# Attention given out in slices of one tile, by running sums of two engines' work, with the norm multiplied on ScalarE

## The chip, the cores and the metric

One core of a Trainium2 chip runs the whole program. Its engines are TensorE (PE: matmuls; PEld is its weight load), VectorE (DVE), ScalarE (ACT), GpSimd (POOL) and SyncE (SP), which here issues nearly all DMAs. Each engine works through its own instructions in the order in which the program issues them to it. The metric is the device time of one execution in microseconds, lower is better.

## What is computed

```python
kv = np.einsum('bhsd,bhse->bhde', k, v)            # 8 batches, 8 heads, 576 rows, 64 features
out = np.einsum('bhsd,bhde->bhse', q, kv)
rms = np.sqrt(np.mean(out * out, axis=-1, keepdims=True) + 1e-06)
x = (out / rms * g_norm)                           # then (B,H,S,D) -> (B*S, H*D): 4608 x 512
h = x @ w_in                                       # 512 x 2048
g = np.maximum(h, 0.0) ** 2
return g @ w_out                                   # 2048 x 512
```

A linear attention, normed per head, feeds a feed-forward block of two matrix products with a squared relu between them. All is fp32; the weights arrive in fp64.

## The kernel before

**Tiles and strips.** The 4608 tokens are 36 tiles of 128 tokens; a batch has 4 full tiles and half of a fifth, which two batches share (the rest tile). Four tiles are a strip, so there are nine strips, 0 to 8. The feed-forward block runs strip by strip: a first half (`up`, x times w_in) and a second half (`down`, g times w_out). Strip 0 multiplies plainly going up; strip 1 goes up in 28 steps of one Strassen product each (`up`, seven products for each of four groups); strips 2 to 8 go up with Strassen twice over, in 55 slots (`up_slot`, `up_small`): seven sets of seven small products, set n starting in slot 7n and its products in every second slot. The second halves have 14 steps (`down`, `down_deep`). The w_in and w_out sums for this are made in strips 0 and 1 by VectorE and GpSimd and streamed back from DRAM in `w_blk` tiles.

**Banks.** Each product of strips 1 to 8 lands in one of three PSUM banks, A, B and C, of a pool of five (`fpsum`). A bank holds several products one after the other, so a product in bank A can only start when the one before it there has been read: by a ScalarE copy (`snap`, line 1153, or 743 in strip 1) or by a VectorE add (line 1148, or 796 in strip 1). In strip 1 the order of the products of a group is 1, 2, 6, 5, 7, 3, 4, of which 1, 6, 7 and 4 use bank A.

**Attention for the coming strips** is cut into slices, a list of functions with arguments that is built once (lines 638 to 689) and worked off by `attend` between the feed-forward's steps. For tiles from batch 2 on, the slices are:

- `transposed_query` (T): VectorE transposes a head pair's queries, line 383, and for the last pair of an odd batch also the rest tile's, line 387. The query is loaded by small DMAs that are let go one at a time (`drip`), at most one in a step, and only where no key load is due; a T whose loads have not yet been issued issues them itself. Each T puts the load of three pairs later on that list.
- `key_value` (K): k times v on PE (line 431), copied to SBUF by ScalarE (lines 436 and 437). Its successor's keys are loaded one or two steps after it.
- `query`: for a pair of tiles, an optional K, then q times kv on PE into two banks `x_ps` (line 467, one buffer), then ScalarE squares the two tiles into SBUF (line 476).
- `mean_roots`: VectorE sums the squares by head (line 484), scales (485), and ScalarE takes the root (490) into a PSUM tile.
- `normalized`: VectorE inverts the root and refines it with one Newton step on tiny operands (lines 495 to 499), then multiplies each of the pair's tiles by it out of PSUM (line 535).
- `squares_x`: VectorE transposes a tile in 32 x 32 blocks (line 602); `send_x` stores it to DRAM, and some steps later `fetch_x` loads it as the feature-major x of a strip.

The first batches go another way: `roots_normalized` does the norm in one slice, and `features` transposes the normed tile on PE (line 595).

**What sets their order.** All engines get their instructions in the order of this one program, so a slice stands on each engine's queue between what the step before it and the step after it issue. In strips 1 to 8 a fixed pace gives the slices out by count: after step i of a strip those up to

```python
pace = 25 if s == DEEP else 36
attend(begun + (goal - begun) * min(i + 1, pace) // pace)
```

where `begun` is the list's place at the strip's start and `goal` the place that the next strip needs (`ready`), or more in later strips. Strip 1 (`DEEP`) works off 24 slices in its first 25 steps, strips 2 to 7 between 13 and 23 each in their first 36 slots.

Of the kernel before, what the change touches and what calls it, by code (L numbers as in the profile page):

```python
# [10 lines left out]
FP32 = mybir.dt.float32  # L11
# [3 lines left out]
AF = mybir.ActivationFunctionType  # L15
ALU = mybir.AluOpType
AX = mybir.AxisListType
# [3 lines left out]
def kernel(  # L21
# [34 lines left out]
    nc = tc.nc  # L56
    P = 128
    B, H, S, D = q.shape
# [3 lines left out]
    NP = H // 2  # L62
# [10 lines left out]
    DEEP = 1  # L73
    DEEP_UP = 2
    SQ = 32
    Q_ON_PE = 2
    X_ON_PE = 2
    EPS = 1e-6
    const = ctx.enter_context(tc.tile_pool(name="const", bufs=1))
# [6 lines left out]
    small = ctx.enter_context(tc.tile_pool(name="small", bufs=3))  # L86
# [10 lines left out]
    apsum = opening.enter_context(tc.tile_pool(name="opsum", bufs=2, space=bass.MemoryType.PSUM))  # L97
# [381 lines left out]
    def mean_of(sqs):  # L479
        ms = small.tile([P, 2, H], FP32, name="ms", tag="ms")[:, : len(sqs)]  # L480
        for i, sq in enumerate(sqs):
            if len(sq.shape) == 3:
                sq = sq.rearrange("p r e -> p (r e)")
            nc.vector.reduce_sum(out=ms[:, i], in_=by_head(sq), axis=AX.X)
        nc.vector.tensor_scalar(out=ms, in0=ms, scalar1=1.0 / D, scalar2=EPS, op0=ALU.mult, op1=ALU.add)
        return ms

    def root_of(ms, ps=None):
        r = ps if ps is not None else small.tile([P, 2, H], FP32, name="rms", tag="rms")[:, : ms.shape[1]]
        nc.scalar.activation(r, ms, AF.Sqrt)  # L490
        return r
# [10 lines left out]
    queried = []  # L502
# [12 lines left out]

    def roots_normalized(ns):
        parts, ms = queried.pop()
        queried.append((parts, (ms, root_of(ms))))
        normalized(ns)

    def mean_roots(ns):
        parts, sqs = queried.pop()
        ms = mean_of(sqs)
        r = apsum.tile([P, 2, H], FP32, name="root", tag="at")[:, : len(ns)]
        queried.append((parts, (ms, root_of(ms, r))))

    def normalized(ns):
        parts, means = queried.pop()
        r = inverse_root(*means)
        for i, n in enumerate(ns):  # L530
            x_n[n] = xn_pool.tile([P, d_model], FP32, name="x_n", tag="x_n")
            o = x_n[n].rearrange("p (q r d) -> p r q d", r=2, d=D)
            x = parts[i].rearrange("p r (q d) -> p r q d", d=D)
            w = r[:, i].rearrange("p (r q) -> p r q", r=2).unsqueeze(3).to_broadcast([P, 2, NP, D])
            nc.vector.tensor_tensor(out=o, in0=x, in1=w, op=ALU.mult)

    first = {}
    TAG_UP = "ABAC"
# [125 lines left out]
    T, K, last = transposed_query, key_value, query_pairs(1)[2]  # L664
    slices += [(query_means, (last,)), (K, (2, 0, 1)), (T, (2, 0)), (roots_normalized, (last,)), (T, (2, 1))]
    slices += [(T, (2, 2)), (features, (last[0],)), (T, (2, 3)), (K, (2, 2, 3))]
    for b in range(2, B):
        pairs = query_pairs(b)
        for i, pair in enumerate(pairs):
            left = len(pairs) - i  # L670
            more = b + 1 < B
            at = left + (b == 2)
            keys = (b + 1, *{2: (0, 1), 1: (2, 3)}[at]) if more and at < 3 else ()
            if i == 0 and b > 2:
                slices += [(T, (b, p)) for p in (2, 3)]
            if i == 0 and b == 3:
                slices.append((K, (3, 2, 3)))
            slices.append((query, (pair, *keys)))
            if more and left == 1:
                slices.append((T, (b + 1, 1)))  # L680
            slices.append((mean_roots, (pair,)))
            slices.append((normalized, (pair,)))
            if more and left == 2:
                slices.append((T, (b + 1, 0)))
            slices += [(squares_x, (n,)) for n in pair]
            for n in pair:
                slices.append((send_x, (n,)))
                if n % NT == NT - 1:
                    ready[n // NT] = len(slices)
    slice_at = [0]  # L690

    def attend(n):
        while slice_at[0] < min(n, len(slices)):
            fn, a = slices[slice_at[0]]
            fn(*a)
            slice_at[0] += 1

    def out_rows(n):

# [486 lines left out]
    for s in range(N_STRIP):  # L1186
# [19 lines left out]
        goal, begun = ready.get(s + 1, len(slices)), slice_at[0]  # L1206
        if s >= DEEP_UP:
            goal = max(goal, min(ready[DEEP_UP] + (len(slices) - ready[DEEP_UP]) * (s - 1) // (N_STRIP - DEEP_UP - 1), len(slices)))
        total, done = sum(w for w, _, _ in steps), 0
        for i, (w, fn, a) in enumerate(steps):  # L1210
            if s == 0 and i < n_up:

                if 4 <= i < 10:
                    convert(3 + i)
                if i == 0:
                    load_next()
                    load_rest(1, nc.sync)
                    load_next()
                if i == 1:
                    load_next()  # L1220
                if i == 2:
                    for b in range(2):
                        load_q_rest(b, nc.sync)
                if i == 14:
                    for b in range(2):
                        store_first(b)
            elif s == 0 and i == n_up:
                convert(len(conversions))
                conv.close()

                stream_pool = ctx.enter_context(tc.tile_pool(name="stream", bufs=4, reuse_waits="tile"))
                sum_pool = ctx.enter_context(tc.tile_pool(name="sum", bufs=8, reuse_waits="tile"))
            if s == 0 and n_up <= i < n_up + 2:
                for g in range(2 * (i - n_up), 2 * (i - n_up) + 2):
                    sum_g1(0, g)
            if s == 0 and n_up + 2 <= i < n_up + 4:
                for g in range(2 * (i - n_up) - 4, 2 * (i - n_up) - 2):
                    sum_g3(0, g)
            fn(*a)
            if s == 0 and i < 4:  # L1240

                convert(3 + i)
            done += w
            if s:
                clock[0] += 3.2 if i >= n_up else 2.2 if s == DEEP else 1.2
                soon = tiles_due and tiles_due[0][2][0] // NT == s + 1
                if i == n_up + 10:
                    while tiles_due and tiles_due[0][2][0] // NT == s + 1:
                        _, f, a = tiles_due.popleft()
                        f(*a)  # L1250
                elif not due(keys_due) and not (soon and due(tiles_due)):
                    least = 2.1 if s == DEEP else 4.5 if i < n_up else 3.3
                    quiet = n_up * 2 // 3 < i < n_up + 3 or s == DEEP and i > n_up + 5
                    if not quiet and clock[0] >= dripped[0] + least:
                        dripped[0] = clock[0]
                        drip(True)
                pace = 25 if s == DEEP else 36
                attend(begun + (goal - begun) * min(i + 1, pace) // pace)
                if s == DEEP and i == n_up - 3:
                    leaf_sums(s, 4)  # L1260
                if s == 1 and i in range(2, 23, 3):
                    deep_sums_in((1, 6, 5, 4, 0, 2, 3)[i // 3])
                if s == 1 and i in (21, 22, 23, 25):
                    stream()
                continue
            if i == n_up:
                stream(2)
            if i in (n_up + 8, n_up + 11):
                load(2, (i - n_up) // 11, nc.sync, "q")
            if i == n_up + 12:  # L1270
                load_q_rest(2, nc.sync)
            if i - n_up in (7, 8, 9, 12):
                sums_in((7, 8, 9, 12).index(i - n_up))
            if i == n_up + 11:
                sums_x(1)
            n = i + 1 - (n_up - 6)
            pairs, m = divmod(max(n - 2 * NP, 0), 3)
            attend(min(ready[0] + min(max(n, 0), 2 * NP) + (n >= 2 * NP) + 4 * pairs + (0, 2, 2)[m], goal))
            if i == n_up + 6:
                stream()  # L1280
            while deep_due and i not in (n_up + 1, n_up + 4):
                store_deep_sums(*deep_due.popleft())
            if i == n_up + 2:
                store_first(2)
                for _ in range(2):
                    load_next(names="kv")
            if i == n_up + 3:
                load_rest(2, nc.sync)
            if 11 <= i < n_up:

                convert((13, 13, 14, 15, 16)[i - 11])
# [30 lines left out]
```

## Time and profile before

| What | Value |
|---|---|
| Median of 3 runs | 897.22 us (895.58 to 900.01) |
| The profiled execution's own time | 894.9 us |
| Its span, first to last instruction | 892.9 us |
| Strip 1, up | from 139.67 us |
| Strip 2, up, to its second half | 239.14 to 294.7 us |
| Norm multiply on VectorE, line 535 | 32 of 686 ns each |
| Sum of squares on VectorE, line 484 | 36 of 674 ns |
| Block transposes on VectorE, lines 602 and 383 | 27 of 695 ns, 24 of 698 ns |
| Root on ScalarE, line 490 (pairs) | 12 of 188 ns, 26.0 us idle before them, waiting for line 485 |

The profile counts an engine as busy from an instruction's start to its end. Matmuls overlap in their pipeline, so one of the second halves shows as 275 ns long while the next begins 112 ns after it; how fast PE moves is read from the starts. The granted TensorE clock was 1.0 throughout. The idle time of an engine is followed by what ended it ("<-"); where that is "issue", the profile shows no releaser.

### The profile page before, as it was taken

The page shows a single profiled execution, that of the slowest core. Times are in us where ns is not written, and L with a number is a line of the kernel's source. Part 1 is how long each engine was busy: PE and PEld are TensorE (multiplying, and loading weights), DVE is VectorE, ACT ScalarE, POOL GpSimd, SP SyncE. Part 2 cuts the span into 40 slices and gives each one's busy share as a digit, 9 for nine tenths or more (in the row PEclk, how much of TensorE's full clock was granted, in tenths as well). Part 3 has the DMA queues.
Part 4 walks back from the last instruction along what each step waited for, and adds up shares of the span by engine and source line. Part 5 has one row for each costly group of instructions (what it writes and reads, how often), then busy time and mean ns, then how long its engine had stood idle before and what let it go on. Part 6 is the DMA issues. An engine that isn't in the chain of part 4 may idle for free.

```text
span 892.9 us, 20684 instructions
## 1 busy us (share of the span) xinstructions
PE 879.6 (99%) x8296; PEld 822.6 (92%) x8296; DVE 733.9 (82%) x1256; ACT 315.6 (35%) x622; POOL 306.7 (34%) x315
## 2 busy tenths in 40 slices
PE   8999999999999999999999999999999999999998
PEld 7445888889999999999999999999999999999998
DVE  4999999779779986898689966895898679866886
ACT  5898242320027202640254023801271027102710
POOL 0000005700548133632373135604470447044700
PEclk9999999999999999999999999999999999999999
DMA  9998997999988798889887979798648965884384
GB/s 311 323 307 256 311 356 236 282 311 324 321 234 241 269 324 231 249 290 317 243 239 238 327 237 248 232 309 283 217 142 293 315 201 160 304 297 155 131 321 174
DMA packets 169231, 235.71 MB, mean 264 GB/s; under 512 B 79408, under 2 KB 134192, under 8 KB 160688
## 3 DMA queue, kind: packets, MB, share of 16 engines
q1 hardware_dynamic: 168976, 234.40, 81.6%
q8 instruction: 65, 1.06, 0.5%
q14 instruction: 30, 0.25, 0.1%
q10 hardware_dynamic: 160, 0.00, 0.0%
HBM read 197.66 MB, written 36.70 MB: 262 GB/s over the span
## 4 chain that ended last, share of the span: by engine, by line
PE 74%; DVE 15%; DMA 6%; issue 3%; ACT 2%; SPq 1%; DVEq 0%; POOL 0%; ACTq 0%; POOLq 0%
PE ps_B L948 22%; PE ps_A L948 17%; PE ps_A L1136 16%; PE ps_B L1136 8%; PE ps_C L1136 4%; DVE w_t L288 2%; PE kv_ps L431 2%; PE x_ps L467 1%; DVE w_c L268 1%; PE ps_A L733 1%; DVE gt L1148 1%; DVE wt L288 1%; DMA w_deep<-w_t 1%; DMA w_blk<-w_deep 1%; DMA raw<-in_moe_w_out_dram 1%
## 5 line engine op out<-in xcount | busy, mean ns | idle before, releaser
L948 PE MATMUL ps_B<-w_blk,g_s 128*128 128x128 f32 x1024 | 126.2, 275 | 0.0
L948 PEld LDWEIGHTS ps_B<-w_blk,g_s 128*128 128x128 f32 x1024 | 120.0, 192 | 0.2
L1136 PE MATMUL ps_A<-x_l,w_in 128*128 128x128 f32 x784 | 104.1, 276 | 0.0
L288 POOL TENSOR_TENSOR x_l<-xT 128x256 f32<-128x256 f32 x21 | 15.4, 733 | 245.4 <-PE ps_A L948 187.5
L948 PE MATMUL ps_B<-w_blk,gt 128*128 128x128 f32 x768 | 97.6, 275 | 0.2 <-DMA w_blk<-w_deep 0.2
L1136 PEld LDWEIGHTS ps_A<-x_l,w_in 128*128 128x128 f32 x784 | 95.4, 192 | 0.5 <-DVE gt L1148 0.2
L948 PE MATMUL ps_A<-w_blk,g_s 128*128 128x128 f32 x768 | 93.6, 275 | 0.0
L948 PEld LDWEIGHTS ps_B<-w_blk,gt 128*128 128x128 f32 x768 | 91.5, 192 | 0.5 <-DMA w_blk<-w_deep 0.4
L948 PEld LDWEIGHTS ps_A<-w_blk,g_s 128*128 128x128 f32 x768 | 89.6, 192 | 0.0
L1148 POOL TENSOR_TENSOR snap<-snap,gt 128x512 f32<-128x512 f32 x35 | 46.6, 1330 | 119.4 <-ACT snap L1153 56.7
L1153 ACT COPY snap<-ps_A 128x512 f32<-128x512 f32 x63 | 36.6, 582 | 133.5 <-PE ps_A L1136 119.5
L1086 ACT ACTIVATE gt<-gt 128x512 f32<-128x512 f32 x112 | 69.6, 622 | 18.0 <-DVE gt L1148 18.0
L963 DVE TENSOR_TENSOR o_sb<-o_sb,ps_B 128x256 f32<-128x256 f32 (+1 forms) x128 | 49.5, 387 | 31.2 <-ACT o_sb L964 23.9
L948 PE MATMUL ps_A<-w_blk,gt 128*128 128x128 f32 x576 | 72.2, 275 | 0.0
L1087 ACT ACTIVATE gt<-gt 128x512 f32<-128x512 f32 x112 | 70.6, 631 | 3.6
L948 PEld LDWEIGHTS ps_A<-w_blk,gt 128*128 128x128 f32 x576 | 68.2, 192 | 0.0
L1148 POOL TENSOR_TENSOR gt<-gt,snap 128x512 f32<-128x512 f32 x42 | 52.5, 1275 | 23.5 <-DVE snap L1148 23.4
L288 DVE TENSOR_TENSOR gt<-gt 128x2048 f32<-128x2048 f32 (+1 forms) x29 | 59.7, 2063 | 0.0
L1046 POOL TENSOR_TENSOR w_i<-w_in 128x512 f32<-128x512 f32 x7 | 10.1, 1450 | 141.3 <-DMA q<-in_q_dram 140.6
L964 ACT COPY o_sb<-ps_A 128x128 f32<-128x128 f32 x24 | 6.4, 265 | 145.8 <-PE ps_A L948 145.8
L1136 PE MATMUL ps_A<-x_l,w_blk 128*128 128x128 f32 x392 | 52.2, 276 | 1.3 <-issue 1.2
L1136 PE MATMUL ps_B<-x_l,w_blk 128*128 128x128 f32 x392 | 52.0, 276 | 0.0
(180 smaller groups left out, 1809.3 us busy)
## 6 DMA issues: line engine op xcount, KB each, us to landing
w_blk<-w_deep SPq DMA_DIRECT2D x56, 1024.0 KB, 6.9
w_blk<-w_out SPq DMA_DIRECT2D x56, 768.0 KB, 6.1
w_blk<-w_in_deep SPq DMA_DIRECT2D x49, 768.0 KB, 5.3
raw<-in_moe_w_in_dram SPq DMA_DIRECT2D x16, 512.0 KB, 6.7
raw<-in_moe_w_out_dram SPq DMA_DIRECT2D x16, 512.0 KB, 6.1
k<-in_k_dram SPq DMA_DIRECT2D x29, 256.0 KB, 4.7
v<-in_v_dram SPq DMA_DIRECT2D x29, 256.0 KB, 5.2
x_d<-x_q SPq DMA_DIRECT2D x27, 256.0 KB, 5.3
```

The lines of the kernel that those rows point to most:

```text
L268: yield nc.vector.scalar_tensor_tensor(out=ci, in0=high, scalar=-(2**30), in1=ci, op0=ALU.bitwise_and, op1=ALU.bitwise_or)
L288: eng.tensor_tensor(out=out, in0=a, in1=b, op=ALU.subtract)
L431: nc.tensor.matmul(ps[ts(h, D), i], lhsT=a, rhs=w, start=i == 0 and c == 0, stop=c == C, skip_group_check=True)
L467: nc.tensor.matmul(ps[half, r, i, ts(p, D)], lhsT=q[row, half], rhs=kvd[b, p][row, row], start=True, stop=True)
L948: nc.tensor.matmul(chain[c][x][:, i, :], lhsT=a[:, f, :], rhs=w[:, f, :], start=x not in opened[c] and f == 0, stop=f == FQ // 2 - 1, skip ...
L963: add = lambda out, a, b: nc.vector.tensor_tensor(out=out, in0=a, in1=b, op=ALU.add)
L1046: nc.gpsimd.tensor_tensor(out=s1, in0=w_half(b, 0, 1), in1=w_half(b, 1, 1), op=ALU.add)
L1086: nc.scalar.activation(o, o, AF.Relu)
L1087: nc.scalar.activation(o, o, AF.Square)
L1136: nc.tensor.matmul(ps[:, i, :], lhsT=w, rhs=rhs, start=j in (1, 2, 5) and i == 0, stop=True, skip_group_check=True)
L1148: add = lambda eng, out, a, b: eng.tensor_tensor(out=out, in0=a, in1=b, op=ALU.add)
L1153: nc.scalar.copy(t, ps)
```

## The change

The slices from batch 2 on become smaller, and in strips 2 to 7 they are given out by two running sums instead of by count.

- `mean_roots` becomes `mean`, one slice for each tile, and `root`. `normalized` becomes `inverse` (the reciprocal and the Newton step) and four slices `scaled_heads`, each for one tile and half of its heads: four ScalarE multiplies of 64 columns out of PSUM, each by one column of norms. The VectorE multiply stays for `roots_normalized` alone (batch 1).
- A tile's block transpose and its store (`squares_x`, `send_x`) follow each other, the first tile's ahead of the last `scaled_heads` of the second. Some query transposes change places: those of pair 0 go ahead of a query, those of pair 1 mostly behind a pair's end.
- `attend_between` replaces the pace in strips 2 to 7. It keeps a sum of pending work for VectorE and for ScalarE: it adds each slot's feed-forward work from `feed_forward_cost` and takes 0.9 off, adds a slice's cost from `ON_DVE` and `ON_ACT`, and takes PE's time in a query off both. In a slot at most one slice for each engine is issued (`root` and `inverse` alone), no more than a pace over 27 slots allows (36 in strip 2), and none that lifts its engine's sum over `BEHIND` while enough slots are left up to slot 38.
- Strip 1 keeps its pace by count over 25 steps; its range of the list now has 34 slices.
- From strip 3 on a strip's goal is rounded to the nearest end of a pair.

```diff
     def roots_normalized(ns):
         parts, ms = queried.pop()
-        queried.append((parts, (ms, root_of(ms))))
-        normalized(ns)
-
-    def mean_roots(ns):
-        parts, sqs = queried.pop()
-        ms = mean_of(sqs)
-        r = apsum.tile([P, 2, H], FP32, name="root", tag="at")[:, : len(ns)]
-        queried.append((parts, (ms, root_of(ms, r))))
-
-    def normalized(ns):
-        parts, means = queried.pop()
-        r = inverse_root(*means)
-        for i, n in enumerate(ns):
+        queried.append((parts, ms))
+        means[ns[0]] = inverse_root(ms, root_of(ms))
+        for i in range(len(ns)):
+            scaled(ns, i)
+
+    means = {}
+
+    def mean(ns, i):
+        parts, sqs = queried[-1]
+        if i == 0:
+            means[ns[0]] = small.tile([P, 2, H], FP32, name="ms", tag="ms")[:, : len(ns)]
+        ms = means[ns[0]]
+        nc.vector.reduce_sum(
+            out=ms[:, i], in_=by_head(sqs[i].rearrange("p r e -> p (r e)") if len(sqs[i].shape) == 3 else sqs[i]), axis=AX.X
+        )
+        if i == len(ns) - 1:
+            nc.vector.tensor_scalar(out=ms, in0=ms, scalar1=1.0 / D, scalar2=EPS, op0=ALU.mult, op1=ALU.add)
+
+    def root(ns):
+        ms = means[ns[0]]
+        means[ns[0]] = ms, root_of(ms, apsum.tile([P, 2, H], FP32, name="root", tag="at")[:, : len(ns)])
+
+    def inverse(ns):
+        means[ns[0]] = inverse_root(*means[ns[0]])
+
+    def place_of(ns, i):
+        parts, n = queried[-1][0], ns[i]
+        if n not in x_n:
             x_n[n] = xn_pool.tile([P, d_model], FP32, name="x_n", tag="x_n")
-            o = x_n[n].rearrange("p (q r d) -> p r q d", r=2, d=D)
-            x = parts[i].rearrange("p r (q d) -> p r q d", d=D)
-            w = r[:, i].rearrange("p (r q) -> p r q", r=2).unsqueeze(3).to_broadcast([P, 2, NP, D])
-            nc.vector.tensor_tensor(out=o, in0=x, in1=w, op=ALU.mult)
+        o = x_n[n].rearrange("p (q r d) -> p r q d", r=2, d=D)
+        return o, parts[i].rearrange("p r (q d) -> p r q d", d=D), means[ns[0]][:, i].rearrange("p (r q) -> p r q", r=2)
+
+    def scaled(ns, i):
+        o, x, w = place_of(ns, i)
+        nc.vector.tensor_tensor(out=o, in0=x, in1=w.unsqueeze(3).to_broadcast([P, 2, NP, D]), op=ALU.mult)
+        if i == len(ns) - 1:
+            queried.pop()
+
+    def scaled_heads(ns, i, r):
+        o, x, w = place_of(ns, i)
+        for p in range(NP):
+            nc.scalar.activation(o[:, r, p], x[:, r, p], AF.Copy, scale=w[:, r, p : p + 1])
+        if i == len(ns) - 1 and r:
+            queried.pop()
 
...
+            if more and left == (1 if b > 2 and b % 2 == 0 else 2):
+                slices.append((T, (b + 1, 0)))
             slices.append((query, (pair, *keys)))
-            if more and left == 1:
+            if left == 1 and b == 2:
                 slices.append((T, (b + 1, 1)))
-            slices.append((mean_roots, (pair,)))
-            slices.append((normalized, (pair,)))
-            if more and left == 2:
-                slices.append((T, (b + 1, 0)))
-            slices += [(squares_x, (n,)) for n in pair]
-            for n in pair:
-                slices.append((send_x, (n,)))
+            slices += [(mean, (pair, t)) for t in range(len(pair))]
+            slices += [(root, (pair,)), (inverse, (pair,))]
+            heads = [(scaled_heads, (pair, t, r)) for t in range(len(pair)) for r in range(2)]
+            slices += heads[:3]
+            for t, n in enumerate(pair):
+                slices += [(squares_x, (n,)), (send_x, (n,))]
                 if n % NT == NT - 1:
                     ready[n // NT] = len(slices)
+                if t == 0:
+                    slices += heads[3:]
+            pair_ends.append(len(slices))
+            if more and left == 1 and b > 2:
+                slices.append((T, (b + 1, 1)))
...
+    ON_DVE = {mean: 0.7, inverse: 0.9, squares_x: 0.67, transposed_query: 0.67}
+    ON_ACT = {query: 1.1, root: 0.2, scaled_heads: 0.9}
+    behind = {ON: 0.0 for ON in ("dve", "act")}
+
+    def feed_forward_cost(slot):
+        dve, act = 2.8 if slot == 5 else 0.0, 0.0
+        for n, p in enumerate(UP_SETS):
+            plain = UP_TO[p][1] is None or p == 5
+            for i, j in enumerate(ORDER):
+                at = 7 * n + 2 * i
+                if at == slot:
+                    if j == 4:
+                        dve += 0.67 * (2 if p == 5 else UP_TO[p][1] is not None)
+                        act += 0.58 * (UP_TO[p][1] is None)
+                    else:
+                        on_act = j == 6 or j in (1, 5) and plain
+                        dve, act = dve + 0.67 * (not on_act), act + 0.58 * on_act
+                if p in FINAL and j not in (1, 6, 5) and at + (5 if p == 5 and j != 4 else 2) == slot:
+                    act += 1.25
+        return {"dve": dve, "act": act}
+
+    def attend_between(slot, begun, goal, first, last):
+
+        for on, cost in feed_forward_cost(slot).items():
+            behind[on] = max(behind[on] - 0.9, 0.0) + cost
+        used, most = set(), begun + -(-(goal - begun) * min(slot + 1, first) // first)
+        while slice_at[0] < most:
+            fn, a = slices[slice_at[0]]
+            on, cost = ("dve", ON_DVE[fn]) if fn in ON_DVE else ("act", ON_ACT.get(fn, 0.0))
+            if fn != send_x:
+                left = sum(f != send_x for f, _ in slices[slice_at[0] : goal])
+                if used and (on in used or fn in (root, inverse) or used & {root, inverse}):
+                    return
+                if left <= last - slot and behind[on] + cost > BEHIND:
+                    return
+                used |= {on, fn}
+            if fn == query:
+                pe = 0.58 * len(a[0]) + (1.6 if len(a) > 1 else 0.0)
+                behind.update({x: max(behind[x] - pe, 0.0) for x in behind})
+            behind[on] += cost
+            attend(slice_at[0] + 1)
 
...
+            if s > DEEP_UP:
+                goal = min(pair_ends, key=lambda end: abs(end - goal))
...
-                pace = 25 if s == DEEP else 36
-                attend(begun + (goal - begun) * min(i + 1, pace) // pace)
+                if s == DEEP:
+                    attend(begun + (goal - begun) * min(i + 1, 25) // 25)
+                elif i < n_up:
+                    attend_between(i, begun, goal, 36 if s == DEEP_UP else 27, 38)
```

`BEHIND` is 1.6. `first` and `last` are the pace and slot 38.

More of the change, by code (lines that the diff above doesn't have):

```diff
@@ L76 @@
     Q_ON_PE = 2
+    BEHIND = 1.6
     X_ON_PE = 2
@@ L666 @@
     slices += [(T, (2, 2)), (features, (last[0],)), (T, (2, 3)), (K, (2, 2, 3))]
+    pair_ends = []
     for b in range(2, B):
```

## The prediction

> **What bounds the kernel now.** I read the engine totals of the page first, then the busy time by stage, then the order of time of TensorE (PE) and VectorE (DVE) where PE is held.
>
> ```profile
> PE 879.6 (99%) x8296; PEld 822.6 (92%) x8296; DVE 733.9 (82%) x1256; ACT 315.6 (35%) x622; POOL 306.7 (34%) x315
> ...
> 520.00:577.60 57.60, 55.48 (x696) 53.94 (x693) 44.92 (x83) 28.23 (x55) 29.63 (x31) 1.00 0.84 235
> ...
> 800.00:847.70 47.70, 47.70 (x430) 47.70 (x429) 32.54 (x48) 23.10 (x42) 29.75 (x32) 1.00 0.45 156
> ```
>
> PE is at 99%. The other two lines are stretches (start:end, length, then busy us of PE, weight load, DVE, ACT, POOL): most of strip 5's first half, and strip 8's, which has no attention. PE is the bound in both, so the change can win only the time in which PE is held, and can lose without limit.
>
> How long PE is held: from strip 2 on a slot of the first half is eight matmul records that begin 0.89 us after the last eight, unless PE waits. I list each slot of strips 2 to 7 that took at least 0.15 us more: strip 2 0.15 and 0.57; strip 4 0.17 and 0.21; strip 5 1.37, 0.25, 0.34, 0.80, 0.35; strip 6 0.82, 0.43, 0.16. Together 5.62 us. Strip 3 and strip 7 have none. The largest, in the timeline of strip 5 (start us, length us, engine and line, what it writes and reads; in brackets the idle time before it and what ended it):
>
> ```profile
> 523.75 1.27 DVE L484 TENSOR_REDUCE ms<-sq 128x8 f32<-128x512 f32 x2
> ...
> 526.46 1.29 DVE L535 TENSOR_TENSOR x_n<-x_ps,newton 128x512 f32<-128x512 f32 x2
> ...
> 527.66 1.25 DVE L963 TENSOR_TENSOR o_sb<-o_sb,ps_B 128x256 f32<-128x256 f32 x3
> ...
> 529.13 1.06 PE L1136 MATMUL ps_B<-xT,w_blk 128*128 128x128 f32 x8
> ...
> 530.02 0.70 DVE L383 STREAM_TRANSPOSE qT<-q 128x512 f32<-128x512 f32 x1
> ...
> 530.64 0.65 DVE L1148 TENSOR_TENSOR snap<-ps_A,gt 128x512 f32<-128x512 f32 x1
> ...
> 531.40 1.13 PE L1136 MATMUL ps_A<-x_l,w_blk 128*128 128x128 f32 x8 [1.21 <-issue]
> ```
>
> DVE does a pair's mean, its norm multiply (L535), the sums of the last strip's output (L963) and a query transpose back to back; the snapshot that empties bank A (530.64) comes after all of them, and PE starts the next product in that bank right after it. The waits are DVE's lump, not DVE's total.
>
> Strip 1, in the same view, is different:
>
> ```profile
> 152.00 0.65 DVE L796 TENSOR_TENSOR gt<-ps_A,snap 128x512 f32<-128x512 f32 x1
> ...
> 152.70 1.99 PE L733 MATMUL ps_A<-x_t,w_in 128*128 128x256 f32 x8 [0.89 <-DVE gt L796]
> ...
> 153.52 1.00 DVE L497 SCALAR_TENSOR_TENSOR newton<-ms,rms 128x8 f32<-128x8 f32 x1
> ...
> 154.76 1.12 DVE L499 SCALAR_TENSOR_TENSOR newton<-newton,rms 128x8 f32<-128x8 f32 x1
> ...
> 155.92 0.69 DVE L535 TENSOR_TENSOR x_n<-x_ps,newton 128x512 f32<-128x512 f32 x1
> ...
> 156.75 0.63 PE L595 MATMUL xt_ps<-ident,x_n 128*128 128x128 f32 x4 [0.33 <-DVE x_n L535]
> ...
> 164.23 0.71 DVE L383 STREAM_TRANSPOSE qT<-q 128x512 f32<-128x512 f32 x1 [2.21 <-DMA q<-in_q_dram]
> ```
>
> DVE is still busy with strip 0's weight sums until 148.27, so at the start of strip 1 DVE is late and PE waits for it: at 152.70 for bank A's release (step 6, product 4), at 156.75 for tile 8's normed x (its transposes are in step 7). At 164.23 DVE itself waits for a query load.
>
> [...] L497 and L499 took 1.00 and 1.12 us while GpSimd ran its weight sums, and 0.17 us at 525.85.
>
> **The change, part by part.**
>
> *The norm multiply goes to ScalarE.* It concerns tiles 9 to 35, 27 tiles: 27 x 0.686 us (L535) = 18.5 us off DVE, 27 x 8 = 216 multiplies of 64 columns onto ACT. Nearest row:
>
> ```profile
> L437 ACT COPY kv_all<-kv_ps 64x64 f32<-64x64 f32 x8 | 1.7, 208 | 0.1
> ...
> L570 ACT ACTIVATE xT<-xt_ps,g_col 128x512 f32<-128x512 f32 x4 | 2.7, 686 | 2.0 <-PE xt_ps L569 2.0
> ...
> L596 ACT COPY xT<-xt_ps 128x512 f32<-128x512 f32 x5 | 2.7, 588 | 5.3 <-PE xt_ps L595 5.3
> ```
>
> No row has a 64-column multiply by a column. Lower bound 0.208 us, the copy; upper 0.31 us, if the column costs the 0.098 us between L570 and L596. A gain below the copy is excluded, since the shape is the same. I take 0.21: 216 x 0.21 = 45 us on ACT, which is idle for half of each first half (28.2 of 57.6 us busy). It costs nothing on PE while ACT's backlog stays under the 2 to 3 slots that a snapshot has before its bank is written again.
>
> *The slices of strips 2 to 7.* I followed the new rule slot by slot with the diff's costs, and put trace durations into the same sum for both versions (0.67 a snapshot or transpose, 0.65 a mean, 0.8 an inverse, 2.8 at slot 5; minus 0.9 a slot, minus PE's own time in a query). Before, DVE's backlog peaks at 5.2 us in strip 4 (slot 10), 5.0 and 4.8 us in strip 5 (slots 9 and 34), 5.2 us in strip 6 (slot 10), and 3.4 and 3.9 us in strips 2 and 3; the held slots of strips 5 and 6 stand at such places. After, the peak is 2.8 us (slot 5, the output sums) in every strip, which strip 8 has now without holding PE; it falls from there and is at most 1.5 from slot 11 on. So the waits of strips 4, 5 and 6 go, 4.90 us, but for two: strip 6's 0.43 is PE waiting for the rest transpose (L387) of the last query transpose, and stays, since that now stands one slot ahead of its query instead of two; for the same reason strip 4 gets one. I take 0.4 more for strip 4 and 0.3 for strip 6 (bounds 0 and 1.2 together). Strip 2's 0.57 at 290.48 is GpSimd slowing the leaf sums at slot 51; no attention is near, it stays. ACT's backlog by the same sum peaks at 3.8 us (strip 5, slot 40) where strip 8 has 2.7 today without a wait. Sum: -(4.90 - 0.43) + 0.7 = -3.8 us, bounds -5.2 and -2.
>
> *Strip 1.* It keeps its pace by count (25 steps), but has 34 slices where it had 24, so the first ones come sooner: tile 8's root and norm in step 2 (was 4), its transposes in step 5 (was 7), query transposes (2,2), (2,3), (3,0) in steps 4, 5, 7 (were 6, 8, 13). DVE's start at 148.27 doesn't move. Its list by step is now: mean 1.15, product 2's two operations 1.95, transpose (2,0) 0.63, inverse 2.63 and norm 0.60 of tile 8, transpose (2,1) 0.65, and only then product 7's add 0.65, which releases bank A: 148.27 + 8.26 = 156.5. PE needs x of tile 8 at the end of step 5, 151.65, but DVE has it at 155.2; the transposes take 0.45, then step 6 waits for bank A: it starts at 156.6, where it started at 152.70. Before, the transposes came later, with a wait of 0.33 and 0.47 of work, and the batch-2 key product (1.46 us) moves from behind to ahead of a step, which is neutral. By step 8 PE is 157.22 -> 160.05 late: +2.8 us. A second way gives the same: transpose (3,0) in step 7 needs its query load. Its halves are issued in steps 6 and 7, behind the key loads, about 163; the trace's landing record of that load before is 166.15, so I take 167. DVE stands until then, with product 2 of step 8 (1.9), two means (1.6) and product 7 of step 11 (0.65) behind it: bank A free at 172.0, where PE's step 13 started at 168.95: +3.1 us. Later in the strip DVE has time to spare (1.1, 2.8 and 1.9 us idle at 179 to 194). At 199 to 200.5 PE now waits 0.6 us for streamed weights, which a later PE need not. Net +2.5 us, bounds +0.5 (GpSimd leaves DVE alone, inverse at 0.8 us, and the load lands at 165) and +5 (it lands at 169.5).
>
> *The rest.* A tile's store is issued in the slot of its transpose, so SP can stand behind DVE for up to 2 us; streamed weights of the first half are issued 22 slots (20 us) ahead, which hides it. A goal rounded to a pair's end never falls short of what the next strip needs: in strips 5 and 6 it lies 3 slices past it, in the others on it. All attention is given out by slot 37, as it was by 36, so the second halves keep theirs. Nothing for these.
>
> Sum: -3.8 + 2.5 = -1.3 us on the profiled 894.9 (span 892.9 and 2.0 around it), so 893.6. The median of the runs shown is 2.3 us higher: 895.9.
>
> **The rivals.** (A) The forecast: both happen, 895.9, own range 893 to 899.5. (B) Strip 1 costs nothing, because GpSimd and the load leave DVE free sooner: 897.2 - 3.8 - 0.6 = 892.8, at best 891 with all of 5.6 won. For it: the bounds above. Against: two separate chains in strip 1 each give 3 us. (C) ScalarE becomes the gate. Place: the three head slices in successive slots of each pair and the DVE transpose behind them. Price: with 0.31 us a multiply, a slice of four is 1.24 us in a slot of 0.89, three of them put ACT 1.05 us behind on top of its copies, DVE then stands for ACT and the bank snapshots behind it; at 0.6 us of PE a pair, 14 pairs give 8.4, so 897.2 + 8.4 + 2.5 - 3.8 = 904.3. It decides from about 0.25 us a multiply. For it: L570 against L596. Against: ACT's idle half, and that PE has two slots of room.
>
> **How the numbers follow.** A 0.55, B 0.2, C 0.25. About 0.5% (4.5 us, below 892.7 or above 901.7) is what a measurement here can tell from no change. Faster is most of B, 0.19; slower is C's most, 0.23; the same 0.58. The range reaches to B's better half and to C's price: 891.5 to 904.
>
> **What would show it.** In strip 1, PE's step 6 (L733 after tile 8's transposes) starting 3 to 4 us later than 152.70 on DVE's x_n or gt, and a DVE wait for q of several us before 167. In strips 4 to 6, slots 0.89 us apart where 1.37, 0.80 and 0.82 stood. The new ACT group of 216 multiplies at 0.21 us. I am wrong if PE waits for ACT snapshots in more than a few slots, or if strip 1's second half starts no later than now.

## The result, and the profile after

The median of 7 runs is 906.78 us (903.28 to 911.09), against 898.45 us (895.58 to 900.52) for the kernel before: a ratio of 1.0097, with a 95% interval of 1.0078 to 1.0117. The change costs 8.3 us. The forecast was 895.9 us, and its range ended at 904.0.

The profiled execution of the changed kernel took 911.1 us, 4.3 above its own median, with a span of 909.1; the profiled one of before, with a span of 892.9, lies 3.6 below its median. The 16.2 us between the two spans are thus about twice the 8.3 between the medians, and what follows tells where they are, not that each of them recurs in every run. I cut both spans at PE's first record (weight loads included) of each half strip:

| Stage | Before, us | After, us | Difference |
|---|---|---|---|
| Strip 0, second half | 55.27 | 59.79 | +4.5 |
| Strip 1, first half | 58.63 | 65.16 | +6.5 |
| Strip 1, second half | 41.70 | 41.09 | -0.6 |
| Strip 2, first half | 55.48 | 55.22 | -0.3 |
| Strip 3, first half | 53.73 | 53.73 | 0 |
| Strip 4, first half | 53.60 | 57.23 | +3.6 |
| Strip 5, first half | 59.71 | 61.61 | +1.9 |
| Strip 6, first half | 54.41 | 53.52 | -0.9 |
| Strips 7 and 8, second halves from strip 2 on | | | 0 |
| After strip 8's first half | 45.43 | 46.70 | +1.3 |

Strip 0's second half is not the change's. Nothing in it was changed, in this execution PE waits there for streamed weights (the 3.4 us below), and over the kernels of this study, which all have the same strip 0, the stage took 54.7 to 60.0 us. The last row's +1.3 comes after PE's last record, which ends 41.3 us after the start of that stage's matmuls in both. What the change did lies in strips 1, 4 and 5. From the page of the changed kernel (share of the span, number of records; PEclk is the granted TensorE clock in tenths; the last line is the new group of multiplies: busy us, mean ns of one, idle before):

```profile
PE 885.1 (97%) x8296; PEld 827.7 (91%) x8296; DVE 719.4 (79%) x1229; ACT 358.9 (39%) x838; POOL 306.3 (34%) x315
...
PEclk9999999899999999999999999999999999999999
...
L560 ACT ACTIVATE x_n<-x_ps,newton 128x64 f32<-128x64 f32 x216 | 47.9, 342 | 11.2 <-DVE newton L500 11.2
```

VectorE has 14.5 us less to do (733.9 before), ScalarE 43.3 us more (315.6 before). PE's share fell from 99% to 97%. PE did not get more work, it has the same 8296 records: it stood for 24.0 us instead of 13.3, and its records took 5.5 us more, which the clock below explains. For what it stood, the list of PE's waits in the changed kernel says (us in total, times, longest us):

```profile
PE kv_ps L432 <- DMA v_rest<-in_v_dram: 3.5, 1, 3.5
PE ps_B L809 <- DMA w_blk<-w_out: 3.4, 1, 3.4
PE x_ps L468 <- DVE qT_rest L388: 3.2, 2, 2.7
PE kv_ps L432 <- DMA v<-in_v_dram: 1.8, 1, 1.8
PE xt_ps L622 <- DVE x_n L553: 1.7, 1, 1.7
...
PE ps_A L809 <- DVE gt L872: 0.5, 1, 0.5
...
PE ps_B L1212 <- DVE snap L1224: 0.4, 1, 0.4
```

The last line is in strip 2, where it stood before as well. The waits for VectorE's snapshots and bank adds that held strips 4 to 6 before are gone. No line of the list names ScalarE. Instead PE waits for three kinds of attention input: a v load, a v_rest load, and a rest query transpose. Strip 1 in the timeline (start us, length us; in brackets the idle time before and what ended it):

```profile
157.39 0.69 DVE L553 TENSOR_TENSOR x_n<-x_ps,newton 128x512 f32<-128x512 f32 x1
158.23 0.63 PE L622 MATMUL xt_ps<-ident,x_n 128*128 128x128 f32 x4 [1.71 <-DVE x_n L553]
158.62 0.65 DVE L872 TENSOR_TENSOR gt<-ps_A,snap 128x512 f32<-128x512 f32 x1
159.33 3.68 PE L809 MATMUL ps_A<-x_t,w_in 128*128 128x256 f32 x8 [0.47 <-DVE gt L872]
...
165.46 0.69 PE L432 MATMUL kv_ps<-v,k 128*64 128x64 f32 x16 [1.83 <-DMA v<-in_v_dram]
166.20 0.71 DVE L384 STREAM_TRANSPOSE qT<-q 128x512 f32<-128x512 f32 x1 [2.80 <-DMA q<-in_q_dram]
166.61 3.46 PE L809 MATMUL ps_A<-xT,w_in 128*128 128x256 f32 x8
```

Before, that key product ran without a gap:

```profile
160.77 1.15 PE L431 MATMUL kv_ps<-v,k 128*64 128x64 f32 x32
```

The first two waits are the ones forecast: x of tile 8, and bank A just after it. The third was not: the key product of batch 2's pairs 2 and 3, moved from step 9 to step 6, is there before its second v load has landed (issued at 158.07, landed at 165.32). And the eight records at 159.33 and at 166.61 take 3.68 and 3.46 us where the same eight take 1.89 in full clock.

Strip 4, PE and VectorE:

```profile
455.33 1.06 PE L1212 MATMUL ps_A<-x_l,w_in 128*128 128x128 f32 x8
...
457.63 0.71 DVE L384 STREAM_TRANSPOSE qT<-q 128x512 f32<-128x512 f32 x1 [2.04 <-DMA q<-in_q_dram]
458.27 0.67 DVE L388 STREAM_TRANSPOSE qT_rest<-q_rest 128x512 f32<-128x512 f32 x1
459.08 0.34 PE L468 MATMUL x_ps<-kv_all,qT_rest 64*64 64x64 f32 x8 [2.69 <-DVE qT_rest L388]
```

PE names the transpose, but VectorE itself had been idle for 2.04 us waiting for the query load (pair 3 of batch 5): a wait behind a wait, and the cause is the DMA. Strip 5:

```profile
556.88 1.15 PE L432 MATMUL kv_ps<-v,k 128*64 128x64 f32 x32
561.52 0.27 PE L432 MATMUL kv_ps<-v_rest,k_rest 64*64 64x64 f32 x2 [3.50 <-DMA v_rest<-in_v_dram]
```

Here it is the v_rest load of batch 7, which SP issued at 553.61 and which landed at 561.39. Before, it was issued at 542.50, landed at 548.03, and its product followed on the key product with no gap:

```profile
548.26 1.15 PE L431 MATMUL kv_ps<-v,k 128*64 128x64 f32 x32
549.34 0.27 PE L431 MATMUL kv_ps<-v_rest,k_rest 64*64 64x64 f32 x2
```

Two things make the 3.5 us. The key product comes 10.2 us after the one that lets the load go, instead of 12.8; and the load itself took 7.78 us instead of 5.53, for a reason that is not shown.

The two idle stretches cost more than their length. The windows of the changed kernel (start:end, length, busy us of PE, weight load, VectorE, ScalarE, GpSimd with their records, then PEclk, DMA share, GB/s):

```profile
456.34:459.75 3.41, 0.72 (x46) 0.70 (x49) 1.88 (x3) 0.00 (x0) 3.33 (x4) 1.00 1.04 283
459.75:463.16 3.41, 3.41 (x47) 3.29 (x38) 1.26 (x2) 1.09 (x2) 0.62 (x2) 0.50 0.90 207
463.16:466.57 3.41, 3.41 (x33) 3.41 (x32) 2.63 (x9) 0.94 (x4) 0.00 (x0) 1.00 0.43 80
...
558.74:562.15 3.41, 0.63 (x38) 0.66 (x42) 0.00 (x0) 0.14 (x1) 0.14 (x1) 1.00 0.61 139
562.15:565.57 3.42, 3.42 (x58) 3.30 (x49) 0.02 (x1) 1.46 (x4) 0.00 (x0) 0.50 0.39 92
```

PE was busy for 0.72 and 0.63 us of one window and got half the clock in the next, for 3.41 us; half of that, 1.7 us each, is as an estimate the lost matmul time. It fits the long records: the eight at 159.33, nearly all in a half window (159.38 to 162.79), took 1.79 us more than in full clock. In the changed kernel it happened at 128.66 (after the weight wait in strip 0), 159.38, 166.20, 459.75, 562.15, and at 906.90; in the kernel before only at 893.66. The last of each comes after PE's last product and costs nothing.

With that the stages add up roughly. Strip 1: waits of 1.71, 0.47 and 1.83 and two half windows of 1.7 make 7.4, less the 0.89 and 0.33 that stood there before, 6.2 (measured +6.5). Strip 4: 2.69 + 1.7 less the 0.38 won, 4.0 (measured +3.6). Strip 5: 3.50 + 1.7 less the 3.1 won, 2.1 (measured +1.9).

The slow clock is not peculiar to the profiled execution. The record has the mean clock of every run: 0.989 to 0.995 in the seven of the changed kernel (mean 0.9923), 0.995 to 1.0 in the 122 of the kernel before that ran with the experiments (mean 0.999). What that costs a run is, as an estimate, the missing share of the clock times the span: 7.0 us against 0.8. Up to some 6 us of the 8.3 are slow clock (less where PE had nothing to do at half rate), and the waits themselves, less what was won, are the smaller part.

### The profile page after: what moved, and what is told of

Read it like the earlier page. It is cut to its first block, busy times and chain, and to the rows that moved or that the text cites. A ratio compares the mean times of both kernels' runs of the same rounds, so it can differ in the third digit from the quotient of the medians.

```text
span 909.1 us, 20900 instructions
## 1 busy us (share of the span) xinstructions
PE 885.1 (97%) x8296; PEld 827.7 (91%) x8296; DVE 719.4 (79%) x1229; ACT 358.9 (39%) x838; POOL 306.3 (34%) x315
## 4 chain that ended last, share of the span: by engine, by line
PE 78%; DVE 9%; DMA 6%; ACT 2%; issue 2%; SPq 1%; POOL 1%; DVEq 0%; POOLq 0%; ACTq 0%
PE ps_B L1024 22%; PE ps_A L1212 18%; PE ps_A L1024 17%; PE ps_B L1212 9%; PE ps_C L1212 5%; PE ps_A L809 2%; DMA w_deep<-w_t 2%; PE kv_ps L432 2%; PE x_ps L468 2%; DVE w_t L289 2%; DVE w_c L269 1%; PE ps_B L809 1%; DVE wt L289 1%; DMA v_rest<-in_v_dram 1%; DMA raw<-in_moe_w_out_dram 1%
## 5 line engine op out<-in xcount | busy, mean ns | idle before, releaser
L560 ACT ACTIVATE x_n<-x_ps,newton 128x64 f32<-128x64 f32 x216 | 47.9, 342 | 11.2 <-DVE newton L500 11.2
```

The lines of the kernel that those rows point to most:

```text
L560: nc.scalar.activation(o[:, r, p], x[:, r, p], AF.Copy, scale=w[:, r, p : p + 1])
```

## The experiments

Two theories stood against each other. L: slices moved ahead of their loads, in three places (strip 1's early slices, the rest keys, the queries of a rest pair). S: ScalarE, which now has 216 multiplies more, is the gate. Each ratio below is to the kernel before, run on the same chip in the same rounds, whose medians were 897.8 to 898.2 us.

**e1_strip1: the change with strip 1's first nine slices in their former steps.**

```diff
-                    attend(begun + (goal - begun) * min(i + 1, 25) // 25)
+                    at = min(i, 24)
+                    attend(begun + (at if at <= 9 else 9 + (goal - begun - 9) * (at - 9) // 15))
```

> The changed kernel, but strip 1 gives out its first nine slices in the steps that they had before the change (the rest in its other 15 steps). Theory L (PE stands idle for loads and for tile 8's x that the new places ask for too early, and after such an idle stretch runs some 3.4 us at half clock): strip 1's first half goes from 65.2 back to about 59 us, no clock window in strip 1, total 906.8 - 5.5 = 901 us. Theory S (ScalarE's 216 small multiplies hold the banks): strip 1 gains little, total 905 to 907.

899.4 us, ratio 1.0013 (0.9998 to 1.0027). Some 7.4 us of the 8.3 come back, and strip 1's first half takes 59.64 us instead of 65.16. Strip 5 went from 61.61 to 57.46 as well, with its wait for v_rest down to 1.1 us, although nothing in it was edited, so the 7.4 is not strip 1's alone. That the loads arrive sooner or later as the strip's start moves against them would explain it, but is not shown. Strip 4 still took 57.07.

**e2_rest: the change with the rest keys loaded two key products earlier.**

```diff
-                if p == NP - 1 and b + 1 < B:
+                if p == 1 and b + 1 < B:
                     keys_later(load_rest, b + 1, nc.sync)
```

> The changed kernel, but the key and value rows of the next batch's rest are loaded after the first key product of a batch instead of the second, some 12 slots sooner. Theory L: the wait of 3.5 us for v_rest in strip 5 falls under 0.6 us and its half-clock window goes: strip 5's first half 61.6 -> 57 us, total about 902 us; strips 1 and 4 as they are. Theory S: no change beyond 1 us.

901.95 us, 1.0044 (1.0026 to 1.0061). PE's waits in this kernel:

```profile
PE kv_ps L432 <- DMA v<-in_v_dram: 2.9, 2, 2.4
PE xt_ps L622 <- DVE x_n L553: 2.5, 1, 2.5
...
PE x_ps L468 <- DVE qT_rest L388: 1.1, 2, 0.6
```

The v_rest wait is 0.3 us (3.5 in the changed kernel), and strip 5 takes 57.17. Strip 1 kept its loss: it took 67.62 us in this execution. What I had not expected: the query wait of strip 4 went too, 57.23 to 53.53. The timeline of SP in the changed kernel shows why:

```profile
448.08 0.66 SPq L162 DMA_DIRECT2D k_rest<-in_k_dram  x1
448.79 0.65 SPq L162 DMA_DIRECT2D v_rest<-in_v_dram  x1
449.47 1.15 SPq L123 DMA_DIRECT2D q<-in_q_dram  x2
...
451.20 0.96 SPq L123 DMA_DIRECT2D q<-in_q_dram  x2
```

Query loads are let go only where no key load is due, and the two rest loads stand just ahead of the late queries. With the rest loads elsewhere, the last of these four query loads went out at 447.67 instead of 451.67, though the strip began only 2.1 us earlier in that execution, and it landed at 450.13. In the changed kernel it landed at 457.55, and the transpose above started at 457.63.

**e3_pace: the change with strips 3 to 7 given out at strip 2's pace.**

```diff
-                attend_between(i, begun, goal, 36 if s == DEEP_UP else 27, 38)
+                attend_between(i, begun, goal, 36, 38)
```

> The changed kernel with a pace over 36 slots in strips 3 to 7 too, instead of 27. Query transpose (5,3) then falls in slot 21 instead of 18, key product (7,0) in slot 24 instead of 22. Theory L: both waits shrink by about 2 to 3 us (2.7 -> 0.5 in strip 4, 3.5 -> 1.5 in strip 5) and one or both half-clock windows go: total about 901 to 903 us. Theory S: ScalarE's work is spread more thinly, a gain of about 2 us spread over all strips, with no single strip standing out.

900.74 us, 1.0027 (1.0015 to 1.0039). Both load waits of strips 4 and 5 are gone in another way, by slices that come later instead of loads that come sooner: 53.47 and 56.40. The total is a little under the 901 to 903 expected, and strip 1 again kept its loss (67.66 us). So it is the order of slice and load that costs, and neither alone.

**e4_heads: the kernel before, with the ScalarE multiplies alone, in the old slice (sixteen in a row for a pair).**

```diff
-            nc.vector.tensor_tensor(out=o, in0=x, in1=w, op=ALU.mult)
+            if n < 9:
+                nc.vector.tensor_tensor(out=o, in0=x, in1=w, op=ALU.mult)
+                continue
+            w = r[:, i].rearrange("p (r q) -> p r q", r=2)
+            for h, p in ((h, p) for h in range(2) for p in range(NP)):
+                nc.scalar.activation(o[:, h, p], x[:, h, p], AF.Copy, scale=w[:, h, p : p + 1])
```

> The kernel before, with one part of the change alone: tiles from 9 on are multiplied by their norms on ScalarE, in eight pieces of 64 columns, in the same slice as before. Theory L: VectorE is 18.5 us lighter and nothing is asked for sooner: 1 to 3 us faster than before (895 to 897). Theory S: ScalarE's 48 us in lumps of two tiles hold the snapshots: 5 us or more slower than before (903 or more).

918.1 us, 1.0219 (1.0183 to 1.0255); L's number was far off, and S's held for this kernel. PE's waits in it:

```profile
PE ps_A L1141 <- ACT snap L1158: 7.8, 5, 3.8
PE ps_A L738 <- ACT snap L748: 4.9, 1, 4.9
...
PE ps_B L1141 <- ACT snap L1158: 1.3, 1, 1.3
```

In lumps of sixteen the multiplies do gate: 14.0 us of PE waiting for ScalarE's snapshots. In fours, the changed kernel has not one such wait. The multiplies keep ScalarE about as long in both (46.0 and 47.9 us), so S is a theory about lumps, and the change's slices avoid it.

**e5_both and e6_three: e1 and e2 together, and these with e3.**

> Both edits together: strip 1's first nine slices in their former steps, and the rest's keys loaded after the first key product of a batch. Theory L: their gains add up (7.4 and 4.8 us off 906.8), 894 to 896 us, and no half-clock window after the start; that is 2 to 4 us faster than before. If the two share a cause (one idle stretch setting off the next), the sum is smaller: 898 or more.

> The same two edits, and the pace over 36 slots in strips 3 to 7 as well. Strips 4 and 5 have little left to win (53.5 and 56.4 us alone against 53.5 and 57.2): 0 to 1 us faster than both edits alone, 893.5 to 896.

898.47 us, 1.0004 (0.9991 to 1.0017), and 897.76 us, 0.9995 (0.9976 to 1.0013): level with before, where I expected 2 to 4 us less. Strips 2 to 7 did deliver in e5: 55.22, 53.73, 53.53, 56.32, 53.52 and 51.13, together 4.6 us under before. Strip 1 gave back 1.8 us of it in e5 (60.45 against 58.63) and 7.0 in e6 (65.65). In e5's execution strip 0's second half also took 60.01 us, which no edit touches; why its median shows no gain is not shown. In e6:

```profile
PE ps_A L809 <- DVE gt L872: 4.5, 2, 3.6
```

VectorE stood for the queries of batch 3's first pair, whose transpose comes in step 10 in these kernels (step 13 before), and bank A's release was queued behind it; half clock followed at 172.76, for two windows.

**e7_dve: e5 with the multiply back on VectorE, one slice a tile.**

```diff
-            heads = [(scaled_heads, (pair, t, r)) for t in range(len(pair)) for r in range(2)]
-            slices += heads[:3]
+            heads = [(scaled, (pair, t)) for t in range(len(pair))]
+            slices += heads[:1]
...
-                    slices += heads[3:]
+                    slices += heads[1:]
...
-    ON_DVE = {mean: 0.7,
+    ON_DVE = {scaled: 0.69, mean: 0.7,
```

> The two edits, but the norm multiply stays on VectorE, one slice for each tile, planned at 0.69 us of VectorE. If the win in strips 4 to 6 comes from the smaller slices and their running sums, this is within 1.5 us of both edits alone (895 to 897). If it comes from VectorE's 18.5 us less work, the DVE waits of strips 5 and 6 come back: 898 to 900.

903.29 us, 1.0054 (1.0033 to 1.0075), worse than e5 by 4.8 us and than both expectations. The rest transposes are late twice, in strips 4 and 6, which take 56.58 and 56.64, each with one half window. The second halves of strips 4 and 5 also lose 1.7 us each, mostly in waits for streamed weights, which these stages do not have in e5's execution.

```profile
PE x_ps L468 <- DVE qT_rest L388: 4.1, 2, 2.0
```

In these slices the multiply on ScalarE is a gain; how much of the 4.8 us is VectorE's load and how much late weights is open.

**e8_fill: e1 with 11 matmuls of no use (2.5 us of work), written into the query's own bank ahead of the query of tiles 22 and 23, which overwrites them.** It adds work that the output doesn't need, at the place where PE stood idle in strip 4.

```diff
+        if ns == [22, 23]:
+            keep_busy(ps[:, 0, 0, 0:P], 11)
```

> Strip 1's former steps alone, and 11 dummy matmuls (2.5 us) ahead of the query of tiles 22 and 23 in strip 4, where PE stood idle for 2.5 us for the rest queries and then ran at half clock for 3.4 us. If standing idle is what halves the clock: the idle time becomes busy at no cost, the granted clock stays full there, and strip 4's first half goes from 57.1 to about 55.4 us (total -1.7 us, 897.7). If the window comes from something else (the load of the other engines, the chip): it stays, 57 us.

898.24 us, 1.0000 (0.9988 to 1.0012), 1.2 us under e1. Strip 4's half window is gone, and the strip went from 57.07 to 55.79, as a half window that no longer follows should do. But in the profiled execution one appeared in strip 5, where v_rest was 2.1 us late instead of 1.1. The stage, 1.28 us shorter, supports the estimate of 1.7 us a window; the total, against e1's interval, cannot settle it.

**e9_place and e10_place_pace: e5 with batch 3's first query transpose back in step 13, and this with e3.**

```diff
-            if more and left == (1 if b > 2 and b % 2 == 0 else 2):
+            if more and b > 2 and left == (1 if b % 2 == 0 else 2):
                 slices.append((T, (b + 1, 0)))
...
+            if b == 2 and left == 2:
+                slices.append((T, (3, 0)))
             slices += heads[:3]
```

> The two edits of the fifth run (strip 1's first nine slices in their former steps, the rest's keys sooner), and query transpose (3,0) back in step 13 of strip 1, behind the pair's inverse, where it stood in step 10 and held VectorE for its load (a PE wait of 1.8 us in that run, 3.6 us and a half-clock window in the sixth). Theory L: strip 1's first half 58.6 to 59.5 us as before the change, strips 2 to 7 some 4.6 us shorter than before: 893 to 895.5 us, 2.5 to 5 us faster than before. If the strip 1 waits come from elsewhere: 897 to 899 as there.

> The same with the pace over 36 slots in strips 3 to 7 as well: within 1 us of it, 893 to 895.5.

896.31 us, 0.9985 (0.9973 to 0.9997), and 896.63 us, 0.9985 (0.9972 to 0.9998): the best kernels of the study, 1.5 us under before, short of the 893 to 895.5 us expected of both. e9's waits:

```profile
PE x_ps L468 <- DVE qT L384: 1.5, 1, 1.5
...
PE x_ps L468 <- DVE qT_rest L388: 1.1, 2, 0.6
```

The first is in strip 1, which still takes 60.64 us, 2.0 more than before; strips 2 to 7 gain 4.0. SP and VectorE in strip 1 of e9 show where the load went:

```profile
156.62 0.61 SPq L162 DMA_DIRECT2D k_rest<-in_k_dram  x1
157.28 0.63 SPq L162 DMA_DIRECT2D v_rest<-in_v_dram  x1
...
158.67 6.09 SPq L123 DMA_DIRECT2D q<-in_q_dram  x6
...
166.45 0.71 DVE L384 STREAM_TRANSPOSE qT<-q 128x512 f32<-128x512 f32 x1 [4.18 <-DMA q<-in_q_dram]
```

The rest loads that e2's edit brings forward now stand ahead of queries in strip 1. The last query load of this transpose goes out 22.3 us after the strip's start, where it went out after 19.7 before, and VectorE stands for it 4.18 us instead of 2.21. PE's wait of 1.53 us for the transpose and 0.36 us inside a key product, for v, are nearly the 2.0 us. No run takes this apart. e5 and e6 have the same order. So has e10 (a wait of 2.1 us in strip 1, 60.81 us); its strips 2 to 7 take 0.6 us less than e9's, and the total is the same.

**e11_early: the kernel before, with only strip 1's first nine slices in the changed kernel's steps.** The multiply, the slices and the pace are those of before.

```diff
-                attend(begun + (goal - begun) * min(i + 1, pace) // pace)
+                attend(begun + max((goal - begun) * min(i + 1, pace) // pace, min(9, 34 * (i + 1) // 25) if s == DEEP else 0))
```

> The kernel before, with one part alone: the first nine slices of strip 1 in the steps that the change gives them (tile 8's norm in step 2 for 4, its transposes in step 5 for 7, key product (2,2) in step 6 for 9); all else as before, transpose (3,0) in step 13 too. Theory L: the waits for x of tile 8, bank A and the v load (together about 3.5 us) and one or two half-clock windows (1.7 us each) appear in strip 1: 63 to 65 us for 58.6, total 902 to 905. If strip 1 was lost through the new slices' work and not through their places: 898 to 899.

907.01 us, 1.0093 (1.0068 to 1.0117), at +9.2 the cost of the whole change, and above the 902 to 905 expected, though strip 1's first half, 64.59 us, is in the range expected for it. Its timeline:

```profile
157.38 0.63 PE L595 MATMUL xt_ps<-ident,x_n 128*128 128x128 f32 x4 [1.58 <-DVE x_n L535]
...
158.49 1.99 PE L733 MATMUL ps_A<-x_t,w_in 128*128 128x256 f32 x8 [0.47 <-DVE gt L796]
...
164.62 1.08 PE L431 MATMUL kv_ps<-v,k 128*64 128x64 f32 x16 [3.52 <-DMA v<-in_v_dram]
```

The same three waits as in the changed kernel, at the same places, and half clock after the third (164.7). With e1, which takes this out of the change and wins 7.4 (with strip 5's part in it), it shows the main cause from both sides.

## Why the prediction was wrong

- **What bounds the kernel, and the gain.** Right. The waits in strips 4 to 6 were VectorE's lump and went; strip 2's 0.57 stayed (that slot again takes 1.46 us, and VectorE's leaf sums at 300.50, 302.19 and 303.87 take 1.15 to 1.16 us beside GpSimd's work on line 1114, 5.09 us from 299.39 on, where the median of each kind is 0.68 to 0.69), and strip 6's rest transpose as 0.55. The term of -3.8 us was good: with the loads in time (e5) strips 2 to 7 gain 4.6.
- **The multiply at 0.21 us.** Right: 47.9 us for 216 is 0.222. The recorded mean of 342 ns would have misled, since the records overlap: 216 of them are 73.9 us, where ScalarE was busy with them for 47.9.
- **Strip 1, +2.5 us: the step that failed, "which is neutral".** The forecast chain is there, but smaller: PE waited 1.71 us for x where the prediction had about 3.5, and with bank A's 0.47 that is 1.0 us more than the 1.22 that stood there before. The second chain is there on VectorE, which stood 6.85 us for the query of (3,0), until 173.76 instead of 167; but PE, late itself, did not wait for it (in e6 it did, 3.6 us). What was missing is the key product: 1.46 us of work moved from behind to ahead of a step, which the prediction called neutral without asking for its v load. That load is issued after the key product before it, and it was late by 1.83 us (3.52 in e11). Two half windows came on top, one after the forecast waits and one after this one. Together +6.5 came out of +2.5.
- **The same step in strips 2 to 7: "The rest. ... Nothing for these."** I summed VectorE's and ScalarE's work slot by slot and looked at stores and streamed weights, but not at the loads that the slices need. In strip 5 the last batch's first key product went from slot 26 to 22, only 9 slots after the one that lets its rest loads go (12 before). In strip 4 the last query transpose of batch 5 went from slot 21 to 18, some 2.7 us sooner, while the last piece of its query load went out 15.9 us after the strip's start where it had gone out after 16.9; the rest loads stand just ahead of it in both kernels. The waits were 3.50 and 2.69 us where the prediction had nothing. e2 and e3 show that either remedy takes them away.
- **The clock.** The prediction priced a wait at its own length. Four half windows in strips 1, 4 and 5, each of 3.41 us at 0.50, added about 7 us in the profiled execution by the estimate of 1.7 us each, close to the 8.0 us of the three load waits themselves. PE was not idle throughout in the windows ahead of them: matmuls filled 1.24, 1.58, 0.72 and 0.63 us of those.
- **The rivals.** C's 904.3 lies nearest to 906.8, but its mechanism is not in the changed kernel, where PE never waits for ScalarE; it is in e4, whose slices are lumps. B ("strip 1 costs nothing") is refuted by e1 and e11. The rival that was missing is a late load.

Open: how much each strip gives of the median's 8.3 us, since stages are read from single executions in which a load may be late by 1 us or by 3. Strip 1 gives most of it: its early slices alone cost 9.2 us (e11), and with them back in their places (e1) 1.2 us are left, with the first halves of strips 2 to 7 at 328.2 us in its profiled execution where they took 328.1 before, so that they neither lost nor won what was forecast.

## What to carry to other kernels

When slices of work are moved, list for each the loads that it needs, what lets them go, and how long they then take (the k, v and q loads named here 2 to 8 us); a slice that comes sooner must bring its load with it, or the wait only changes its name. A list that lets loads go one at a time makes each load late that is put behind another, so a late transpose can be cured by moving a load of something else, as in strip 4 of e2, and another one made late by it, as in strip 1 of e9. And price a stand of TensorE of two microseconds or more at its length plus the slow clock that may follow it, here 3.41 us at 0.50, some 1.7 us of matmul time by the estimate above.

## What the runs showed of the hardware

In the changed kernel half clock came after windows in which PE stood for as little as 1.83 us of 3.41. The windows lie on a grid: the six starts at half clock named above (128.66 to 906.90) are 9, 2, 86, 30 and 101 times 3.413 us apart. I cut PE's time into windows on this grid. In the changed kernel half clock followed windows with 2.70, 2.18, 1.83, 2.69 and 2.79 us of idle time, and the sixth came after PE's last product; between PE's first and last product no other window had more than 1.09. In the kernel before the most was 1.21 us, from 528.44 on, and full clock followed it.

In windows at half clock, less idle time went with a second one. The five of the changed kernel in which PE still had products had no idle time in them, and the full clock came back; with 0.50, 0.61, 1.11 and 1.50 us, in e2, e3, e6 and e4, a second half window followed. In e2:

```profile
161.80:165.21 3.41, 2.91 (x27) 2.53 (x28) 0.65 (x1) 0.52 (x2) 3.25 (x3) 0.50 1.15 271
165.21:168.63 3.42, 3.42 (x9) 2.70 (x9) 0.06 (x1) 0.59 (x1) 0.78 (x2) 0.50 0.96 239
```

Where PE stands 1.53 us in a stretch of 3.40 us, in e9, the clock stays:

```profile
163.90:167.30 3.40, 1.87 (x57) 1.35 (x59) 0.71 (x1) 0.59 (x1) 3.32 (x3) 1.00 1.11 266
167.30:170.70 3.40, 3.40 (x30) 3.00 (x31) 0.96 (x2) 1.08 (x2) 3.24 (x4) 1.00 0.77 208
```

In e10 a stand of 2.06 us, from 166.69, fell over two windows, 1.85 us of it in the first, and the clock stayed too, while in e7 two stands of 2.05 us, at least 2.02 us of each in one window, were followed by half clock. Of these three stands of nearly the same length, the one that fell over two windows kept the full clock, and the two that fell into one lost, by the estimate, 1.7 us more each.
